# Attention into a gated MLP on one core: a new opening for the first head pair, and other places for two weight conversions

## Chip, core and metric

The kernel runs on 1 core of one Trainium2 chip. The metric is the device time of one execution in microseconds (us); lower is better. Times of the kernel before: 728.61, 730.03 and 730.19 us, median 730.03.

## What is computed

Rotary attention for 4 batches of 8 heads, 576 positions and head size 64, then a gated MLP on the result, all in FP32:

```python
q_rot, k_rot = (rotate(q), rotate(k))
scores = scale * np.matmul(q_rot, k_rot.transpose(0, 1, 3, 2))
scores = scores - np.max(scores, axis=-1, keepdims=True)
attn = np.exp(scores)
attn = attn / (np.sum(attn, axis=-1, keepdims=True) + 1e-09)
attn_out = np.matmul(attn, v)
...
x = np.ascontiguousarray(attn_out.transpose(0, 2, 1, 3)).reshape(B * S, H * D)
g = x @ w_gate
out = (g * (1.0 / (1.0 + np.exp(-g))) * (x @ w_val)) @ w_out
```

w_gate and w_val are 512 by 1536 float64 arrays, w_out 1536 by 512; the kernel reads their 64-bit words and converts them on the chip.

## The kernel before

The 32 heads are taken as 16 pairs. A pair's scores make 9 blocks of 128 queries by 576 keys: blocks 0 to 7 are four row groups i times the two heads h, block 8 holds the last 64 queries of both heads. Over all pairs the blocks are numbered n = 0 to 143, so n = 9 begins the second pair; here pairs are counted from 0.

**Per pair.** SP loads X (q and k, line 169) and VR (v, line 180). POOL turns q and k into rot (`turn`, lines 202 to 204). PE transposes rot (lines 281 and 285), ACT casts it to the high part of N (line 300), DVE subtracts to get the low part (line 304). FP32 products are made of three terms of high and low parts. SP then copies N into stacked tiles QK, QZ and BD (`qk_stack`, lines 311 to 318), which put a high and a low part in one contraction of 128 rows.

**Per block.** PE makes the scores (line 341): a block listed in `PLAN["direct"]` reads N alone, with 64 rows, three terms and six matmuls; any other of blocks 0 to 7 reads QK and QZ, with four. DVE takes the row maximum (`peak`, line 356), ACT the exponential (line 374), PE transposes E (line 417), ACT and DVE split it (lines 418 and 419), PE multiplies with the split v in VS (line 457), ACT evacuates (line 462) and SP stores Y (lines 476 to 482). The score tile sc has two buffers, so the scores of block n+2 wait for the exponential of block n. POOL makes VS from VR (`vsplit`, lines 270 and 271); VR has one buffer.

**The first weight block.** While attention runs, `wfirst(0, i)` loads a [128, 1024] piece of w_gate (i = 0) or w_val (i = 1) into a tile R (line 745) and `bits10` converts it in nine steps: ACT takes the absolute value (line 727), DVE makes four passes (lines 728 to 731), ACT casts the high part (line 703), DVE makes a fifth pass (line 732), POOL subtracts and adds (lines 705 and 706). R has one buffer; attention's row sums, too, are read back into R (line 611, from block 42 on).

**What sets the order.** `start` is written out by hand. Warming products (line 225, identity times identity into an unused tile) stand between its PE instructions, their counts in PLAN["warm"]. After it a loop over n calls one step function after another in PLAN["order"]; PLAN["cv"] holds, for each weight half, the n of the load and then of its nine steps. PE keeps program order while n < 9, SP while n < 27, POOL always; elsewhere a scheduler places the instructions. Each engine, and SP's queue of DMA starts, works strictly in the order shown.

After attention come the MLP's products: a plain part, a part with seven products in place of eight, and the down projection.

Of the kernel before, what the change touches and what calls it, by code (L numbers as in the profile page):

```python
# [24 lines left out]
NFF = DFF // 128  # L25
QH = 1216
PLAN = dict(
    direct=[0, 1, 2, 3, 4, 5, 9, 10],
    trb=3,
    warm=[10, 2, 2, 3, 2, 3],  # L30
    order=["qk", "scores", "trans", "pv", "exp", "evac", "rstore", "rope", "tails", "conv", "x", "conv1", "vsplit"],
    qk=[[3, 4, 6], [1, 2, 3], [0, 0, 1]],
    qkw=[[0, 2, 1], [2, 0, 1], [2, 0, 1]],
# [5 lines left out]
    rope=1,  # L39
    vsplit=8,  # L40
    rstore=0,
    cv=[[13, 16, 17, 21, 22, 23, 25, 25, 26, 26], [27, 29, 30, 30, 31, 32, 34, 34, 35, 35]],
    xs=[[4, 6], [5, 5], [6, 5], [7, 5], [8, 7], [9, 5], [10, 5], [11, 5], [12, 7], [13, 7], [14, 1], [14, 2],
        [14, 8], [15, 0], [15, 2], [15, 4]],
    xe=[[5, 3], [6, 3], [7, 3], [8, 3], [9, 3], [10, 3], [11, 3], [12, 3], [13, 5], [14, 1], [14, 3], [14, 5],
# [50 lines left out]
def r32(ap):  # L96
    return ap.bitcast(FP32)
# [10 lines left out]
class Attn:  # L108
# [103 lines left out]
    def start(self):  # L212
        nc = self.nc
        ve, po = nc.vector, nc.gpsimd
        rot = self.rot[0] = self.rot_p.tile([128, NSLOT, D], FP32, name="rot")
        rf = rot.rearrange("p s d -> p (s d)")
        T = nc.tensor.transpose
        tr = lambda: self.tr_p.tile([128, 512], FP32, name="tr")
        hi = lambda *x: self.qk_hi(0, *x)
        lo = lambda *x: self.qk_lo(0, *x)  # L220
        pw = self.pv_p.tile([128, 512], FP32, name="pv")

        def warm(n):
            for _ in range(n):
                nc.tensor.matmul(pw[:, 0:128], self.ident, self.ident, start=True, stop=True)  # L225
        w = PLAN["warm"]
        nc.scalar.copy(self.et_p.tile([128, 640], FP32, name="Et")[:, 0:1], r32(self.BD[0])[:, 0, 0:1])
        warm(w[0])
        self.turn(po, 0, 2)
        self.turn(ve, 0, 1, 0, 4, False)  # L230
        nc.scalar.mul(self.tab[0], self.tab[1], float(D ** -0.5))
        self.turn(ve, 0, 0, 0, 1)
        self.turn(po, 0, 0, 1, 4)
        pk, pt, pq = tr(), tr(), tr()
        kt = lambda i: T(pk[:, i * 128:(i + 1) * 128], rf[:, 512 + i * 128:640 + i * 128], self.ident)
        for o in (64, 0):
            T(pt[:, o:o + 128], rf[:, 1024:1152], self.ident)
        warm(w[1])
        for i in range(4):
            kt(i)  # L240
        warm(w[2])
        T(pq[:, 0:128], rf[:, 0:128], self.ident)
        for x in ((pt, None, 192), (pk, 640, 512), (pq, 64, 128)):
            hi(*x)
        for x in ((pt, None, 192), (pk, 640, 512), (pq, 64, 128)):
            lo(*x)
        nc.scalar.copy(self.VS[0][:, :, 0:64], self.VR)
        warm(w[3])
        self.scores(0, False, lambda x: warm(w[4]) if x == 0 else None)
        self.peak(0)  # L250
        self.scores(1, False)
        self.peak(1)
        self.exp(0)
        ps = tr()
        for i in range(1, 4):
            T(ps[:, i * 128:(i + 1) * 128], rf[:, i * 128:(i + 1) * 128], self.ident)
        warm(w[5])
        hi(ps[:, 128:512], 192, 384)
        lo(ps[:, 128:512], 192, 384)
        self.exp(1)  # L260
        del self.rot[0], self.X[0]
        self.load_qk(2)
        self.qk_stack(0)
# [56 lines left out]
    def scores(self, n, peak=True, then=None):  # L320
        nc = self.nc
        p, blk = divmod(n, 9)
        QK, BD, N = (t[p % 2] for t in (self.QK, self.BD, self.N))
        ps = self.sc_p.tile([128, 1024], FP32, name="sc").rearrange("p (a b) -> p a b", a=2)
        self.sc[n] = ps
        if n in PLAN["direct"]:
            i, h = divmod(blk, 2)
            sl = slice(64 + i * 128, 192 + i * 128)
            hs, ko = slice(64 * h, 64 * h + 64), (640, 576)[h]
            terms = [(N[hs, x, sl], N[hs, y], ko) for x, y in ((1, 1), (0, 1), (1, 0))]  # L330
        elif blk < 8:
            i, h = divmod(blk, 2)
            sl = slice(64 + i * 128, 192 + i * 128)
            ko = (640, 576)[h]
            QZ = self.QZ[p % 2]
            terms = [(QK[:, h, 0, sl], QK[:, h, 1], 0), (QZ[:, h, i * 128:(i + 1) * 128], N[:, 0], ko)]
        else:
            terms = [(BD[:, 1], N[:, 1], 640), (BD[:, 0], N[:, 1], 640), (BD[:, 1], N[:, 0], 640)]
        for x, (l, rr, o) in enumerate(terms):
            for g in range(2):  # L340
                nc.tensor.matmul(ps[:, g, 0:288], l, rr[:, o + g * 288:o + (g + 1) * 288],  # L341
                                 start=(x == 0), stop=(x == len(terms) - 1))
            if then:
                then(x)
        if peak:
            self.peak(n)
# [619 lines left out]
def attn_swiglu(ctx: ExitStack, tc: tile.TileContext, qk, vr, wg, wv, wo, main, tail, out):  # L966
# [6 lines left out]
    NB = NP * 9  # L973
# [4 lines left out]
    at = Attn(tc, actx, early, scx, qk, vr, (main, tail), yd, rd)  # L978
    ve, po = nc.vector, nc.gpsimd
# [17 lines left out]

    @step
    def scores(n, p, b):
        if 1 < n + 1 < NB:  # L1000
            at.scores(n + 1)

    @step
# [3 lines left out]

    @step
    def exp(n, p, b):
        if 1 < n + 1 < NB:  # L1010
            at.exp(n + 1)

    @step
# [66 lines left out]
    for n in range(NB):  # L1080
        p, b = divmod(n, 9)
        if n == 9:
            ctl1.__exit__(None, None, None)
        if (p, b) == (NP - 1, 0):
            assert not cvq
            early.close()
            moe.open_early(mctx)
        if n == 27:
            ctl0.__exit__(None, None, None)
        if b == P["lqk"] and 0 < p < NP - 3:  # L1090
            at.load_qk(p + 3)
        if b == P["lv"] and 0 < p < NP - 1:
            at.load_v(p + 1)
        for name in P["order"]:
            steps[name](n, p, b)
            if name == "qk" and n == P["qk"][0][2]:
                at.load_v(1)
                at.load_qk(3)
    assert not pend and not xq
    ctl2 = tc.manual_schedule(engines={getattr(mybir.EngineType, e) for e in ("PE", "Activation", "DVE", "SP")})  # L1100
# [4 lines left out]
    ps = [moe.mm(0, 0, 0, 0)]  # L1105
# [9 lines left out]
    ps = [moe.mm(0, 0, 1, 0)]  # L1115
# [258 lines left out]
```

## Time and profile before

| | |
|---|---|
| median of 3 runs | 730.03 us |
| profiled execution, its own time | 730.19 us |
| its span (first to last instruction) | 728.4 us |
| PE (TensorE) busy | 702.2 us, 96% |
| DVE (VectorE), POOL (GpSimd), ACT (ScalarE) busy | 542.7, 468.1, 408.7 us |
| DMA | 143.86 MB, mean 198 GB/s |

The profile is of one execution. All positions are us from the span's start, and lie 1.79 us short of that execution's own time. PE's ends are modelled, and its 128-column FP32 products show as two records each.

### The profile page before, as it was taken

To read this page: it belongs to the slowest core of one execution; us is meant where nothing else is said; L and a number is where in the kernel's file an instruction comes from. 1 tells how busy PE (TensorE), PEld (TensorE's weight loads), DVE (VectorE), ACT (ScalarE), POOL (GpSimd) and SP (SyncE) were. 2 spreads that over 40 slices of the span, in tenths; PEclk is the share of its full clock that TensorE was granted. 3 is DMA by queue.
4 is the path that set the end of the run, shared out by engine and by line. 5 is a ranking of instruction groups with operands and counts; after the bars stand their busy time and mean duration, and the time that the engine had idled before them with its cause. 6 is when DMAs were issued, how large, how long until landed. Compare 5 with 4: busy or idle time off the path is not lost.

```text
span 728.4 us, 12775 instructions
## 1 busy us (share of the span) xinstructions
PE 702.2 (96%) x4360; PEld 659.8 (91%) x4360; DVE 542.7 (75%) x888; ACT 408.7 (56%) x889; POOL 468.1 (64%) x469
## 2 busy tenths in 40 slices
PE   7979999999999999998999999999999999999997
PEld 7878889999999999997989999999999977888887
DVE  5878888898888889657988878777766894456451
ACT  4778788888888888446553434424334342343331
POOL 7885679999999966585976765556764857200000
PEclk9999999999999999999999999999999999999999
DMA  5787877879888878783346564755547974687661
GB/s 169 189 224 188 229 181 197 224 211 238 214 210 209 217 195 243 181 254 137 106 142 194 169 189 135 202 164 174 160 140 216 312 267 161 275 266 269 204 216 30
DMA packets 111329, 143.86 MB, mean 198 GB/s; under 512 B 17808, under 2 KB 86048, under 8 KB 111264
## 3 DMA queue, kind: packets, MB, share of 16 engines
q1 hardware_dynamic: 106576, 137.64, 65.8%
q10 hardware_dynamic: 4688, 5.39, 2.3%
q8 instruction: 35, 0.57, 0.3%
q14 instruction: 30, 0.25, 0.1%
HBM read 76.35 MB, written 42.54 MB: 163 GB/s over the span
## 4 chain that ended last, share of the span: by engine, by line
PE 67%; DMA 11%; DVE 7%; ACT 6%; POOL 3%; issue 3%; SPq 2%; ACTq 0%; POOLq 0%; DVEq 0%
PE ch L816 28%; PE ch L933 13%; PE pv L457 8%; PE sc L341 7%; PE tr L417 6%; PE ch L884 3%; DMA HF<-hf 2%; DMA QK<-N 2%; ACT E L374 2%; DMA raw<-in_moe_w_gate_dram 2%; DMA raw<-in_moe_w_val_dram 1%; DMA ht<-sv 1%; PE tr L281 1%; ACT N L300 1%; PE pv L225 1%
## 5 line engine op out<-in xcount | busy, mean ns | idle before, releaser
L356 DVE TENSOR_REDUCE nmt<-sc 128x1 f32<-128x576 f32 x144 | 108.0, 751 | 23.8 <-PE sc L341 22.7
L374 ACT ACTIVATE E<-sc,nmt 128x576 f32<-128x576 f32 x128 | 97.2, 759 | 4.2 <-DVE nmt L356 3.2
L417 PE MATMUL tr<-ident,E 128*128 128x128 f32 x512 | 77.6, 275 | 1.0 <-DVE ET1l L419 0.7
L800 POOL TENSOR_TENSOR u<-u,z 128x384 f32<-128x384 f32 x30 | 30.5, 1017 | 72.9 <-DVE sg L800 72.9
L417 PEld LDWEIGHTS tr<-ident,E 128*128 128x128 f32 x512 | 61.5, 141 | 4.1 <-PE tr L281 1.6
L341 PE MATMUL sc<-QK 128*128 128x288 f32 x240 | 59.1, 327 | 3.2 <-ACT E L374 1.9
L819 ACT COPY c<-ch 128x384 f32<-128x384 f32 x30 | 14.4, 480 | 84.7 <-PE ch L816 46.1
L202 POOL TENSOR_TENSOR t<-X,tab 128x256 f32<-128x256 f32 (+2 forms) x94 | 53.7, 593 | 5.9 <-DVE rot L204 3.4
L418 ACT CAST ET2h<-tr 128x512 fp32r<-128x512 f32 x80 | 47.0, 588 | 16.4 <-PE tr L417 16.0
L676 DVE TENSOR_TENSOR hl<-hg,hh 128x384 fp32r<-128x384 f32 x44 | 26.2, 595 | 38.9 <-ACT hh L676 38.9
L419 DVE TENSOR_TENSOR ET2l<-tr,ET2h 128x512 fp32r<-128x512 f32 x80 | 53.1, 681 | 2.1 <-ACT ET2h L418 2.0
L933 PE MATMUL ch<-Oh,hh 128*128 128x512 f32 (+1 forms) x144 | 54.0, 375 | 0.0
L933 PE MATMUL ch<-Oh,hl 128*128 128x512 f32 (+1 forms) x144 | 53.9, 374 | 0.0
L933 PE MATMUL ch<-Ol,hh 128*128 128x512 f32 (+1 forms) x144 | 53.8, 374 | 0.0
L341 PE MATMUL sc<-N,QZ 128*128 128x288 f32 x240 | 51.6, 297 | 0.0
L419 DVE TENSOR_TENSOR ET1l<-tr,ET1h 128x512 fp32r<-128x512 f32 x64 | 42.9, 685 | 9.3 <-ACT ET1h L418 9.0
L204 POOL TENSOR_TENSOR rot<-rot,t 128x512 f32<-128x512 f32 (+2 forms) x47 | 47.0, 999 | 3.7
L203 POOL TENSOR_TENSOR rot<-X,tab 128x512 f32<-128x512 f32 (+2 forms) x47 | 47.0, 1001 | 0.0
L676 ACT CAST hh<-hg 128x384 fp32r<-128x384 f32 x44 | 22.6, 513 | 41.4 <-DVE hg L920 41.4
L800 DVE TENSOR_TENSOR sg<-ch,u 128x384 f32<-128x384 f32 x60 | 33.4, 557 | 16.3 <-PE ch L816 13.3
L418 ACT CAST ET1h<-tr 128x512 fp32r<-128x512 f32 x64 | 36.6, 596 | 14.7 <-PE tr L417 14.5
L457 PE MATMUL pv<-ET2h,VS 128*128 128x320 f32 x128 | 41.1, 331 | 3.9 <-ACT ET2h L418 3.7
(414 smaller groups left out, 2415.9 us busy)
## 6 DMA issues: line engine op xcount, KB each, us to landing
QK<-N SPq DMA_DIRECT2D x64, 288.0 KB, 4.8
hg<-ht SPq DMA_DIRECT2D x22, 768.0 KB, 6.7
HF<-hf SPq DMA_DIRECT2D x12, 896.0 KB, 5.3
X<-in_qk_dram SPq DMA_DIRECT2D x15, 576.0 KB, 5.4
yd<-Y SPq DMA_DIRECT2D x31, 256.0 KB, 3.3
ht<-sg SPq DMA_DIRECT2D x20, 384.0 KB, 3.8
hf<-sg SPq DMA_DIRECT2D x20, 384.0 KB, 3.4
ht<-sg SPq DMA_DIRECT2D x20, 320.0 KB, 3.0
```

The costliest lines, as they stand in the source:

```text
L202: e.tensor_tensor(out=sel(t2, u), in0=sel(x, w), in1=tb(Sn, u), op=ALU.mult)
L341: nc.tensor.matmul(ps[:, g, 0:288], l, rr[:, o + g * 288:o + (g + 1) * 288], start=(x == 0), stop=(x == len(terms) - 1))
L356: nc.vector.tensor_reduce(out=nmcol, in_=ps[:, :, 0:288], axis=AX.XY, op=ALU.max, negate=True)
L374: nc.scalar.activation(out=E.rearrange("p (a b) -> p a b", a=2), in_=ps[:, :, 0:288], func=ACTF.Exp, bias=nmcol, scale=1.0, accum_out=self ...
L417: nc.tensor.transpose(ps[:, c], E[:, o + c * 128:o + (c + 1) * 128], self.ident)
L418: nc.scalar.copy(dst[0], src)
L419: nc.vector.tensor_tensor(out=dst[1], in0=src, in1=r32(dst[0]), op=ALU.subtract)
L457: nc.tensor.matmul(st["ps"][:, 0:w], VS[:, sl, :], t, start=(x == 0), stop=(x == last))
L676: return [lambda: self.nc.scalar.copy(h, f), lambda: le.tensor_tensor(out=l, in0=f, in1=r32(h), op=ALU.subtract)]
L800: add = lambda e, out, in0, in1: e.tensor_tensor(out=out, in0=in0, in1=in1, op=ALU.add)
L816: nc.tensor.matmul(acc, l[:, w, c * 128:(c + 1) * 128], r, start=(n == 0), stop=(n == 5))
L933: self.nc.tensor.matmul(ps, l[:, f], r[:, z], start=(n == 0), stop=(n == 3 * NFF - 1))
```

## The change

- The start's second row group of q gets its own turn on POOL (slots 1 to 2, then 2 to 4), its own transpose, cast and low part; row groups 2 and 3 follow after the scores of block 2, which move, with their exponential, from the loop into `start`.
- The warming counts go from 10, 2, 2, 3, 2, 3 (22 products) to 9, 0, 1, 2, 0, 1 (13).
- In directly read blocks the term (q high, k low) comes before (q low, k high).
- Block 11 is read directly from N. It is the one new entry of that table.
- The load of pair 1's v comes ahead of that pair's stacking copies on SP (n = 5), no longer behind them.
- The w_gate piece is loaded at n = 9 in place of 13, and its steps stand at n = 14 to 27 (before 16 to 26). The w_val piece is loaded at n = 29 (before 27), its steps at 33 to 41 (before 29 to 35).

```diff
--- before.py
+++ after.py
@@ -25,9 +25,9 @@
 NFF = DFF // 128
 QH = 1216
 PLAN = dict(
-    direct=[0, 1, 2, 3, 4, 5, 9, 10],
+    direct=[0, 1, 2, 3, 4, 5, 9, 10, 11],
     trb=3,
-    warm=[10, 2, 2, 3, 2, 3],
+    warm=[9, 0, 1, 2, 0, 1],
     order=["qk", "scores", "trans", "pv", "exp", "evac", "rstore", "rope", "tails", "conv", "x", "conv1", "vsplit"],
     qk=[[3, 4, 6], [1, 2, 3], [0, 0, 1]],
     qkw=[[0, 2, 1], [2, 0, 1], [2, 0, 1]],
@@ -39,7 +39,7 @@
     rope=1,
     vsplit=8,
     rstore=0,
-    cv=[[13, 16, 17, 21, 22, 23, 25, 25, 26, 26], [27, 29, 30, 30, 31, 32, 34, 34, 35, 35]],
+    cv=[[9, 14, 16, 17, 21, 22, 22, 25, 27, 27], [29, 33, 34, 35, 39, 39, 40, 40, 41, 41]],
     xs=[[4, 6], [5, 5], [6, 5], [7, 5], [8, 7], [9, 5], [10, 5], [11, 5], [12, 7], [13, 7], [14, 1], [14, 2],
         [14, 8], [15, 0], [15, 2], [15, 4]],
     xe=[[5, 3], [6, 3], [7, 3], [8, 3], [9, 3], [10, 3], [11, 3], [12, 3], [13, 5], [14, 1], [14, 3], [14, 5],
@@ -230,7 +230,8 @@
         self.turn(ve, 0, 1, 0, 4, False)
         nc.scalar.mul(self.tab[0], self.tab[1], float(D ** -0.5))
         self.turn(ve, 0, 0, 0, 1)
-        self.turn(po, 0, 0, 1, 4)
+        self.turn(po, 0, 0, 1, 2)
+        self.turn(po, 0, 0, 2, 4)
         pk, pt, pq = tr(), tr(), tr()
         kt = lambda i: T(pk[:, i * 128:(i + 1) * 128], rf[:, 512 + i * 128:640 + i * 128], self.ident)
         for o in (64, 0):
@@ -248,16 +249,21 @@
         warm(w[3])
         self.scores(0, False, lambda x: warm(w[4]) if x == 0 else None)
         self.peak(0)
+        T(pq[:, 128:256], rf[:, 128:256], self.ident)
         self.scores(1, False)
         self.peak(1)
+        hi(pq[:, 128:256], 192, 128)
         self.exp(0)
+        lo(pq[:, 128:256], 192, 128)
+        self.exp(1)
+        warm(w[5])
+        self.scores(2)
         ps = tr()
-        for i in range(1, 4):
+        for i in range(2, 4):
             T(ps[:, i * 128:(i + 1) * 128], rf[:, i * 128:(i + 1) * 128], self.ident)
-        warm(w[5])
-        hi(ps[:, 128:512], 192, 384)
-        lo(ps[:, 128:512], 192, 384)
-        self.exp(1)
+        hi(ps[:, 256:512], 320, 256)
+        lo(ps[:, 256:512], 320, 256)
+        self.exp(2)
         del self.rot[0], self.X[0]
         self.load_qk(2)
         self.qk_stack(0)
@@ -327,7 +333,7 @@
             i, h = divmod(blk, 2)
             sl = slice(64 + i * 128, 192 + i * 128)
             hs, ko = slice(64 * h, 64 * h + 64), (640, 576)[h]
-            terms = [(N[hs, x, sl], N[hs, y], ko) for x, y in ((1, 1), (0, 1), (1, 0))]
+            terms = [(N[hs, x, sl], N[hs, y], ko) for x, y in ((1, 1), (1, 0), (0, 1))]
         elif blk < 8:
             i, h = divmod(blk, 2)
             sl = slice(64 + i * 128, 192 + i * 128)
@@ -997,7 +1003,7 @@
 
     @step
     def scores(n, p, b):
-        if 1 < n + 1 < NB:
+        if 2 < n + 1 < NB:
             at.scores(n + 1)
 
     @step
@@ -1007,7 +1013,7 @@
 
     @step
     def exp(n, p, b):
-        if 1 < n + 1 < NB:
+        if 2 < n + 1 < NB:
             at.exp(n + 1)
 
     @step
@@ -1087,6 +1093,8 @@
             moe.open_early(mctx)
         if n == 27:
             ctl0.__exit__(None, None, None)
+        if n == 5:
+            at.load_v(1)
         if b == P["lqk"] and 0 < p < NP - 3:
             at.load_qk(p + 3)
         if b == P["lv"] and 0 < p < NP - 1:
@@ -1094,7 +1102,6 @@
         for name in P["order"]:
             steps[name](n, p, b)
             if name == "qk" and n == P["qk"][0][2]:
-                at.load_v(1)
                 at.load_qk(3)
     assert not pend and not xq
     ctl2 = tc.manual_schedule(engines={getattr(mybir.EngineType, e) for e in ("PE", "Activation", "DVE", "SP")})
```

**PE, first instructions of the program.** pv<-ident are the warming products, tr<-ident,rot transposes of q and k, sc<-N the directly read scores (six to a block), tr<-ident,E those of block 0. Before:

```order
L225 MATMUL pv<-ident 128x128 x10
L237 MATMUL tr<-ident,rot 128x128 x2
L225 MATMUL pv<-ident 128x128 x2
L235 MATMUL tr<-ident,rot 128x128 x4
L225 MATMUL pv<-ident 128x128 x2
L242 MATMUL tr<-ident,rot 128x128
L225 MATMUL pv<-ident 128x128 x3
L341 MATMUL sc<-N_93 128x288 x2
L225 MATMUL pv<-ident 128x128 x2
L341 MATMUL sc<-N_93 128x288 x10
L256 MATMUL tr<-ident,rot 128x128 x3
L225 MATMUL pv<-ident 128x128 x3
L341 MATMUL sc<-N_93 128x288 x6
L417 MATMUL tr<-ident,E 128x128 x4
```

Now:

```order
L225 MATMUL pv<-ident 128x128 x9
L238 MATMUL tr<-ident,rot 128x128 x2
L236 MATMUL tr<-ident,rot 128x128 x4
L225 MATMUL pv<-ident 128x128
L243 MATMUL tr<-ident,rot 128x128
L225 MATMUL pv<-ident 128x128 x2
L347 MATMUL sc<-N_93 128x288 x6
L252 MATMUL tr<-ident,rot 128x128
L347 MATMUL sc<-N_93 128x288 x6
L225 MATMUL pv<-ident 128x128
L347 MATMUL sc<-N_93 128x288 x6
L263 MATMUL tr<-ident,rot 128x128 x2
L423 MATMUL tr<-ident,E 128x128 x4
```

The scores of block 0 have two warming products just ahead of them and none inside; the last two transposes of q stand behind the scores of block 2 instead of ahead of them.

**SP, around the load of w_gate.** The names with 93 to 96 belong to even pairs, those with 113 to 116 to odd ones. Before, behind the stacking copies of pair 2:

```order
L318 DMA BD_95<-N_93 64x2x64
L180 DMA VR<-in_vr_dram 128x640
L481 DMA yd_57<-Y_538 128x2x256
L482 DMA yd_57<-Y_538 128x2x64
L745 DMA R<-in_moe_w_gate_dram 128x1024
L618 DMA Xab<-yd_57 64x2x384
L476 DMA yd_57<-Y_672 128x2x256
```

Now, behind those of pair 1:

```order
L324 DMA BD_115<-N_113 64x2x64
L169 DMA X<-in_qk_dram 128x1152
L482 DMA yd_57<-Y_401 128x2x256
L169 DMA X<-in_qk_dram 128x1152
L751 DMA R<-in_moe_w_gate_dram 128x1024
L317 DMA QK_94<-N_93 64x2x576
L318 DMA QK_94<-N_93 64x2x576
```

The load stands ahead of pair 2's eight stacking copies and of pair 3's load of v.

**SP, around the load of w_val and the stacking copies of pair 4.** Before:

```order
L618 DMA Xab<-yd_57 64x2x384 x2
L476 DMA yd_57<-Y_923 128x2x256
L313 DMA QZ_96<-N_93 64x512
L316 DMA QZ_96<-N_93 64x512
L317 DMA BD_95<-N_93 64x2x64
L745 DMA R<-in_moe_w_val_dram 128x1024
L318 DMA BD_95<-N_93 64x2x64
L180 DMA VR<-in_vr_dram 128x640
L311 DMA QK_94<-N_93 64x2x576
L312 DMA QK_94<-N_93 64x2x576
```

Now:

```order
L624 DMA Xab<-yd_57 64x2x384 x2
L180 DMA VR<-in_vr_dram 128x640
L482 DMA yd_57<-Y_924 128x2x256
L751 DMA R<-in_moe_w_val_dram 128x1024
L319 DMA QZ_96<-N_93 64x512
L322 DMA QZ_96<-N_93 64x512
L323 DMA BD_95<-N_93 64x2x64
L324 DMA BD_95<-N_93 64x2x64
L317 DMA QK_94<-N_93 64x2x576
L318 DMA QK_94<-N_93 64x2x576
```

The loads of VR and of w_val now stand ahead of all eight copies.

## Rows read from the trace of the kernel before

**Rows 1.** The page's busy table: each engine's busy time, share of the span and instructions.

```profile
PE 702.2 (96%) x4360; PEld 659.8 (91%) x4360; DVE 542.7 (75%) x888; ACT 408.7 (56%) x889; POOL 468.1 (64%) x469
```

**Rows 2.** Stretch table of three pairs: length; busy us (instructions) by engine; clock; DMA; GB/s.

```profile
49.60:73.40 23.80, 18.22 (x133) 17.27 (x131) 17.24 (x30) 17.26 (x42) 15.03 (x17) 0.93 0.74 201
73.40:94.40 21.00, 18.97 (x137) 16.82 (x135) 18.02 (x32) 16.12 (x40) 13.52 (x15) 1.00 0.73 199
110.70:127.20 16.50, 16.38 (x132) 15.97 (x130) 14.44 (x24) 14.61 (x38) 15.78 (x19) 1.00 0.75 187
```

**Rows 3.** Timeline of PE, 50 to 89 us: start, length, what [idle before <-releaser].

```profile
54.24 0.46 PE L457 MATMUL pv<-ET2h,VS 128*128 128x320 f32 x1 [3.69 <-ACT ET2h L418]
...
72.15 0.63 PE L417 MATMUL tr<-ident,Et 128*128 128x128 f32 x4 [1.54 <-DVE ET2l L419]
...
88.39 0.42 PE L341 MATMUL sc<-QK 128*128 128x288 f32 x2
```

**Rows 4.** Timeline of ACT, 52 to 81 us.

```profile
53.05 0.66 ACT L727 ACTIVATE R<-R 128x512 f32<-128x512 f32 x1 [4.10 <-DMA R<-in_moe_w_gate_dram]
...
69.19 0.68 ACT L703 CAST w0h<-R 128x512 fp32r<-128x512 f32 x1
...
80.20 0.67 ACT L727 ACTIVATE R<-R 128x512 f32<-128x512 f32 x1 [1.65 <-DMA R<-in_moe_w_val_dram]
```

**Rows 5.** Stretch table around PE's longest stop and at the start.

```profile
54.20:57.70 3.50, 3.19 (x12) 2.89 (x13) 2.92 (x5) 2.82 (x8) 3.42 (x4) 0.54 0.78 236
3.00:6.75 3.75, 3.70 (x17) 3.70 (x18) 1.43 (x4) 0.78 (x2) 1.88 (x5) 1.00 1.00 352
6.75:8.75 2.00, 2.00 (x20) 2.00 (x19) 1.65 (x6) 0.67 (x2) 0.35 (x1) 1.00 0.31 127
```

**Rows 6.** Timeline of SP's queue, 30 to 82 us.

```profile
33.01 0.41 SPq L169 DMA_DIRECT2D X<-in_qk_dram  x1
38.01 0.60 SPq L311 DMA_DIRECT2D QK<-N  x1
...
47.52 0.52 SPq L745 DMA_DIRECT2D R<-in_moe_w_gate_dram  x1
...
75.00 1.53 SPq L745 DMA_DIRECT2D R<-in_moe_w_val_dram  x1
...
80.56 1.47 SPq L315 DMA_DIRECT2D QK<-N  x1
```

**Rows 7.** Stretch table of DVE's instructions on tile R alone.

```profile
49.60:73.40 23.80, 3.05 (x5) 0.93 0.74 201
73.40:94.40 21.00, 3.32 (x5) 1.00 0.73 199
```

**Rows 8.** Chain of waits, 0 to 45 us: start, length, what.

```profile
8.92 0.67 PE pv L225 x6
...
10.05 0.64 PE pv L225 x4
...
12.23 0.83 ACT E L374 x2
13.07 0.37 ACT N L300
...
17.41 5.63 DMA QK<-N
...
23.18 0.77 PE sc L341 x4
...
27.99 0.99 PE sc L341 x6
...
34.37 0.53 PE sc L341 x4
```

**Rows 9.** Timeline of POOL, 8 to 72 us.

```profile
8.40 1.14 POOL L202 TENSOR_TENSOR t<-X,tab 128x192 f32<-128x192 f32 x2 [3.44 <-DVE rot L204]
...
71.33 1.30 POOL L706 TENSOR_TENSOR w0l<-R 128x512 fp32r<-128x512 f32 x1
```

## Prediction

> **What bounds the kernel now.** The page's busy table comes first: PE is busy for 702.2 us of the span, 96%, no other engine above 75% [rows 1]. So nearly every microsecond in which PE stops is a microsecond of the total, and work put on another engine costs nothing until PE waits for it. The next view is the stretch table, cut where pairs end. An undisturbed pair takes 16.5 us for 132 PE instructions, 0.125 us each; DVE is busy for 14.44 us of it [rows 2]. Two early stretches stand out: 23.8 us for 133 instructions, where 16.6 would do, and 21.0 us for 137, where 17.1 would do [rows 2]. They lost 7.2 and 3.9 us. These are the pairs in which w_gate and w_val are converted.
>
> The timelines say how. PE stood still for 3.69 us up to 54.24, released by ACT [rows 3]; ACT had itself stood for 4.10 us in front of the absolute value of w_gate, whose data had not landed [rows 4]. SP had only started that load at 47.52, 5.5 us before it was used [rows 6]. PE then ran at a mean granted clock of 0.54 from 54.2 to 57.7 [rows 5], which costs 3.5 x (1 - 0.54) = 1.6 us more: of its two levels it was mostly at 1.2 GHz in place of 2.4, after that stop. The second stop is 1.54 us before 72.15, behind DVE's low part [rows 3]; the cast of w_gate, 0.68 us, had just been put in front of the casts of that chain on ACT [rows 4]. Together 3.69 + 1.6 + 1.54 = 6.8 of the 7.2 us. In the next stretch ACT stood again, 1.65 us, for w_val, started at 75.00 [rows 4, 6], while DVE had 3.32 us of passes over R to do [rows 7] and was busy for 18.02 of 21.0 us [rows 2].
>
> **The change, step by step.** The sum is made against the profiled execution's 730.19 us, 0.16 above the median of 730.03.
>
> *The load of w_gate.* It now stands on SP right behind the load of X that started at 33.01 and took 0.41 [rows 6], so it starts near 33.5 and, with the same 5.5 us, lands near 39; two X loads ahead of it may make that 41. Its first step stands eleven ACT instructions earlier than before. It was reached at 53.05 - 4.10 = 48.95 [rows 4]; eleven instructions of some 0.55 us put it near 43. The wait is gone and with it the fall of the clock: -3.69 - 1.6 = -5.3. The cast stands a few blocks earlier, and the casts of the 72.15 chain keep the order of an undisturbed pair: -1.5.
>
> *The load of w_val and its steps.* The load keeps about its place in time, but its first step is four blocks later, n = 33 in place of 29; a block is 16.5 / 9 = 1.8 us, so the wait of 1.65 goes. All nine steps leave the 21.0 us stretch but the first three: -3.9 for that stretch, what comes back being the next item.
>
> *The DVE passes, now spread.* Ten passes of 3.05 + 3.32 = 6.4 us [rows 7] lie over four pairs, 1.6 each, where an undisturbed pair leaves 16.5 - 14.44 = 2.06 [rows 2]. The lower bound is 0. The upper is the 21.0 us stretch without its 1.65: 2.25 lost for 3.32 of passes, 0.68 per us, 4.3 in all. I take 2.0, under the middle, since each pair stays within its room: +2.0.
>
> *Block 11 read directly.* Six matmuls take 0.99, the four stacked ones 0.53 [rows 8]: +0.46. What it covers: the load of v ahead of pair 1's copies makes SP wait for POOL's `vsplit` and puts those copies back, by 0.7 at most as I estimate. Block 11 no longer needs them, and block 12 comes a block, 1.8 us, later. I cost the moved load at 0; without block 11's change it would cost up to 0.7.
>
> *The start.* One product less ahead of block 0's scores (0.67 for three [rows 8]), two less ahead of k's transposes, two less inside the scores (0.64 [rows 8]): block 0's exponential, at 12.23, comes about 1.2 earlier, at 11.0, and, being 0.83 long, ends near 11.85 [rows 8]. The scores of block 2 need its buffer and take 0.99, to 12.85. Only then come the transposes of q's last two row groups and their cast, some 0.8 together, to 13.65. Before, the one cast of all three groups ended at 13.07 + 0.37 = 13.44 [rows 8]. The stacking copies wait for exactly that cast; their chain ends with a copy started at 17.41 that took 5.63 us, and PE took up the scores of block 7 at 23.18, on its landing [rows 8]. So what PE gains at the start it loses in front of blocks 6 and 7, and the copies start 0.2 later: +0.2. Bounds: -0.7 if the cast comes 0.5 earlier and the 0.2 is saved as well, +1.5 if block 0 gains nothing, or the clock stays low there (below). POOL's split turn is four more instructions, where the two of rows 9 took 1.14: some 0.8 us, covered by its idle time (15.03 busy of 23.8 [rows 2]); uncovered it would be 0.8. The changed order of the two terms is worth at most tenths there, and stands in these bounds.
>
> Sum: -5.3 - 1.5 - 3.9 + 2.0 + 0.46 + 0.2 = -8.0, so 730.19 - 8.0 = **722.1 us**. Everything behind the sixth pair keeps its order and moves up whole.
>
> **The clock at the start.** From 3.0 to 6.75 PE got through 17 product records in 3.70 us, from 6.75 on through 20 in 2.0 [rows 5], so it begins at half speed even though the clock column reads 1.00 there. Nine of the 22 products that kept PE busy are gone, and between 7 and 9 us transposes and pauses replace most of them. By the rows the clock is lost after a stop of 3.69 us, not after one of 1.54 [rows 3, 5], and the new pauses are about 1 us: I let it stay at 2.4 GHz. The Trainium skill, page "TensorE: Matmul & The Clock Gate", part 4 on PE-mode transpose, says that transposes do not count as PE being busy in the way products do. By that rule the start would run at 1.2 GHz for longer, the second rival below; no row of this trace separates the two, since products stood between all transposes.
>
> **Rivals.**
> 1. *DVE gives back all of it.* For: DVE lost PE time in the 21.0 us stretch. Against: it then had all five passes of a half in one pair. 722.1 + 2.3 = 724.4 us.
> 2. *The clock stays low at the start.* Six us at half speed cost 3; half is hidden ahead of blocks 6 and 7, the rest makes the cast late: 722.1 + 1.5 = 723.6 us.
> 3. *The first load still lands late*, so that the change doesn't do what it is arranged for: SP may stand at the X load ahead of it, which waits for POOL. Against: a margin of 2 to 4 us. With the whole stop left, 722.1 + 5.3 = 727.4 us.
> 4. *SP stands at the w_val load, and the kernel is slower.* That load needs R, which POOL frees with its last step on w_gate; that ended at 72.63 before [rows 9] and, PE being 6.8 us earlier and a `vsplit` now ahead of it, should end near 67. Behind the load stand all eight copies of pair 4. From the load to the last copy read by block 37 took 5.56 us [rows 6]; with the rest of the issue and 5.63 to land that is 80. Pair 4's scores began at 88.39 [rows 3] and now come near 79.5, block 37 near 81: just in time. Every us by which POOL is later than 67 stops PE for about as long, and a long stop costs the 1.6 of clock too. From 73.5 on the whole gain is gone; at 75 it is 722.1 + 8 + 1.6 = 731.7 us. Against: POOL waited before for ACT's cast, which now comes five blocks ahead of POOL's step.
>
> The words of the change speak of three more unstacked blocks; the table gains one, block 11, and I priced one. Two more would be 0.9 us.
>
> **How the numbers follow.** Forecast 0.66, rivals 0.12, 0.10, 0.06 and 0.06. The range goes from 718.8 (nothing given back, 2.0; the start's lower bound, 0.9 below my value; the last 0.4 of the 7.2) to 727.0 (give-back and start both at their upper bounds make 725.7; short of rival 3 in full). A measurement of this kernel tells 0.2%, 1.5 us, from no change. Faster by more: 0.66 + 0.12 + 0.10 and most of rival 3, 0.92. Within: 0.04, the ends of rivals 3 and 4. Slower: 0.04, the rest of rival 4.
>
> **What would show it.** Right: no ACT wait on either weight load; the pair that took 23.8 us near 17; the clock column at 1.00 all through 40 to 70; block 7 beginning within 0.5 us of 23.2 behind a wait for QK of 1 to 2 us; DVE above 90% busy in four pairs with PE stops under 1 us; the last pairs and the MLP 8 us earlier and otherwise alike. Wrong: a PE stop over 3 us left anywhere before 110, block 7 much earlier than 23 us, or pairs 1 to 4 each losing over 1 us to DVE.

## Result and the profile after

The changed kernel takes 722.17 us (median of 4 runs, 720.41 to 724.69) against 730.11 us (4 runs, 728.61 to 733.0): a ratio of 0.9889, with a 95% interval from 0.9842 to 0.9936, so 1.1% faster. Run again it gave 723.00 us (6 runs) against 730.28 us (11 runs), ratio 0.9898 [0.9864, 0.9931]. The forecast was 722.1. The sum came out; not all of its terms did, and this section shows which.

The profiled execution took 723.66 us, its span 721.8, 6.6 less than before's 728.4. The line of the busy table that answers to [rows 1]:

```profile
PE 698.6 (97%) x4344; PEld 656.6 (91%) x4344; DVE 540.0 (75%) x889; ACT 410.0 (57%) x890; POOL 470.5 (65%) x473
```

PE still bounds the kernel. To see where the time went, both traces are cut at the same piece of work: the start of each pair's block 8, the only one read from the tile BD. Four pairs of before, from pair 1's block 8 to pair 5's (stretch table, columns as in [rows 2]):

```profile
43.36:65.88 22.52, 18.43 (x131) 17.27 (x130) 15.98 (x27) 15.40 (x38) 15.55 (x18) 0.92 0.84 212
65.88:85.87 19.99, 17.06 (x131) 15.95 (x130) 15.88 (x27) 16.16 (x40) 14.28 (x16) 1.00 0.78 216
85.87:104.00 18.13, 17.49 (x131) 16.14 (x131) 17.15 (x31) 15.86 (x41) 11.73 (x15) 1.00 0.62 158
104.00:121.42 17.42, 16.82 (x132) 16.03 (x131) 14.36 (x24) 14.69 (x38) 14.39 (x17) 1.00 0.90 227
```

The same four of the changed kernel:

```profile
43.84:60.98 17.14, 16.68 (x131) 15.90 (x130) 15.52 (x26) 15.64 (x39) 13.21 (x16) 1.00 0.82 202
60.98:78.59 17.61, 16.87 (x131) 16.02 (x130) 16.38 (x28) 15.58 (x39) 12.86 (x16) 1.00 0.91 233
78.59:99.69 21.10, 18.38 (x133) 17.61 (x131) 16.31 (x28) 15.48 (x39) 15.93 (x18) 0.92 0.78 209
99.69:116.56 16.87, 16.55 (x131) 15.93 (x130) 15.51 (x27) 15.45 (x39) 15.73 (x19) 1.00 0.89 214
```

The first pair gives back 5.4 us and has its full clock; the second 2.4. The third is a surprise: 3.0 us longer than before, with the clock down. The whole span, with a second profile of each kernel (among the experiments below), in us:

| stretch | before | before, 2nd | after | after, 2nd |
|---|---|---|---|---|
| start to pair 0's block 8 | 25.41 | 25.96 | 25.67 | 25.69 |
| to pair 1's | 17.95 | 17.96 | 18.17 | 18.16 |
| to pair 2's | 22.52 | 22.66 | 17.14 | 17.14 |
| to pair 3's | 19.99 | 19.99 | 17.61 | 18.13 |
| to pair 4's | 18.13 | 18.14 | 21.10 | 19.12 |
| to pair 5's | 17.42 | 17.83 | 16.87 | 16.88 |
| to the MLP's first plain product | 167.39 | 168.23 | 167.59 | 166.60 |
| to the end | 439.59 | 439.43 | 437.65 | 437.78 |
| span | 728.4 | 730.2 | 721.8 | 719.5 |

The surprise stands in the timeline of PE of the changed kernel (source lines from L234 on are numbered one to eight higher than before: L341 is L347, L745 is L751):

```profile
65.45 0.50 PE L347 MATMUL sc<-QK 128*128 128x288 f32 x2 [0.67 <-ACT Et L383]
...
82.31 0.50 PE L347 MATMUL sc<-QK 128*128 128x288 f32 x2 [2.32 <-DMA QK<-N]
```

At 82.31 begins block 36, the first of pair 4, behind a stop of 2.32 us for its stacked copies. The stretch table around it:

```profile
80.00:82.00 2.00, 0.00 (x0) 0.00 (x0) 0.35 (x1) 1.33 (x4) 1.92 (x3) 1.00 1.02 226
82.00:84.00 2.00, 1.69 (x13) 1.72 (x14) 0.88 (x2) 0.45 (x1) 1.92 (x3) 0.94 0.91 202
84.00:86.00 2.00, 2.00 (x11) 2.00 (x10) 1.98 (x6) 1.44 (x6) 1.84 (x5) 0.50 1.01 332
86.00:88.00 2.00, 2.00 (x15) 1.98 (x14) 1.24 (x2) 0.69 (x3) 2.00 (x3) 0.71 0.67 237
```

PE did nothing from 80 to 82, and the granted clock read 0.50 from 84 to 86, the lower of its two levels, only some 2 us after PE had taken up work again: 2 x 0.50 + 2 x 0.29 + 2 x 0.06 = 1.7 us lost behind a stop of 2.32. The DMA share beside it is 1.02, so the 16 engines had no room left while the copies were under way. SP's queue shows what stood ahead of them:

```profile
69.24 0.35 SPq L180 DMA_DIRECT2D VR<-in_vr_dram  x1
69.68 0.38 SPq L482 DMA_DIRECT2D yd<-Y  x1
71.90 0.33 SPq L751 DMA_DIRECT2D R<-in_moe_w_val_dram  x1
72.28 0.82 SPq L319 DMA_DIRECT2D QZ<-N  x1
...
75.93 0.59 SPq L318 DMA_DIRECT2D QK<-N  x1
...
78.14 0.86 SPq L321 DMA_DIRECT2D QK<-N  x1
```

SP stands before the w_val load until 71.90, and all eight copies of pair 4 stand behind it. SP's own waits, and POOL's timeline, which says when R came free:

```profile
SPq L624 <- DMA yd<-Y: 3.0, 1, 3.0
SPq L751 <- POOL w0l L712: 1.8, 1, 1.8
```

```profile
66.82 0.72 POOL L276 TENSOR_SCALAR VS<-VR 128x640 fp32r<-128x640 f32 x1 [4.20 <-DMA VR<-in_vr_dram]
67.63 1.58 POOL L277 TENSOR_TENSOR VS<-VR,VS 128x640 fp32r<-128x640 f32 x1
69.16 1.32 POOL L711 TENSOR_TENSOR R<-R,w0h 128x512 f32<-128x512 f32 x1
70.56 1.31 POOL L712 TENSOR_TENSOR w0l<-R 128x512 fp32r<-128x512 f32 x1
```

POOL's last step on w_gate ends at 71.87, and SP goes on at 71.90. POOL was not waiting for ACT's cast any more, as it did in before's order; it stood 4.20 us at `vsplit`, for v, which is now ahead of those two steps. This is the chain of waits that the fourth rival of the prediction names. Whether it also sets the length of PE's stop is asked below.

At the start the changed kernel is where it was: block 7 begins at 23.20 (before 23.18 [rows 8]). PE, then ACT:

```profile
7.55 1.11 PE L236 MATMUL tr<-ident,rot 128*128 128x128 f32 x4
...
16.64 0.66 PE L287 MATMUL tr<-ident,rot 128*128 128x128 f32 x4 [0.60 <-POOL rot L204]
...
22.35 0.66 PE L287 MATMUL tr<-ident,rot 128*128 128x128 f32 x4 [0.51 <-POOL rot L204]
23.20 0.50 PE L347 MATMUL sc<-QK 128*128 128x288 f32 x2 [0.18 <-DMA QK<-N]
```

```profile
11.68 0.74 ACT L380 ACTIVATE E<-sc,nmt 128x576 f32<-128x576 f32 x1 [0.27 <-DVE nmt L362]
...
14.07 0.37 ACT L306 CAST N<-tr 128x256 fp32r<-128x256 f32 x1 [0.32 <-PE tr L263]
```

The four transposes of k take 1.11 us; between warming products, in the kernel before, they took 0.60. So PE is still at the lower level there, and exp(0) comes only 0.55 us earlier than the 12.23 of [rows 8]; the late cast ends at 14.44, a microsecond after before's 13.44.

### The profile page after: what moved, and what is told of

It reads as the page before. It is cut to its first block, busy times and chain, and to the rows that moved or that the text cites. A ratio compares the mean times of both kernels' runs of the same rounds, so it can differ in the third digit from the quotient of the medians.

```text
span 721.8 us, 12739 instructions
## 1 busy us (share of the span) xinstructions
PE 698.6 (97%) x4344; PEld 656.6 (91%) x4344; DVE 540.0 (75%) x889; ACT 410.0 (57%) x890; POOL 470.5 (65%) x473
## 4 chain that ended last, share of the span: by engine, by line
PE 71%; DMA 10%; DVE 8%; ACT 6%; issue 2%; SPq 2%; POOL 1%; ACTq 0%; DVEq 0%; POOLq 0%
PE ch L822 26%; PE ch L939 13%; PE pv L463 10%; PE sc L347 9%; PE tr L423 7%; DMA HF<-hf 3%; PE ch L774 2%; PE tr L287 2%; DMA raw<-in_moe_w_gate_dram 2%; DMA QK<-N 2%; ACT E L380 1%; DMA ht<-sv 1%; DVE HF L880 1%; POOL fl L682 1%; DVE nmt L362 1%
## 5 line engine op out<-in xcount | busy, mean ns | idle before, releaser
L347 PE MATMUL sc<-QK 128*128 128x288 f32 x238 | 58.5, 327 | 4.2 <-DMA QK<-N 2.5
L424 ACT CAST ET2h<-tr 128x512 fp32r<-128x512 f32 x80 | 47.1, 588 | 16.5 <-PE tr L423 16.2
L347 PE MATMUL sc<-N,QZ 128*128 128x288 f32 x238 | 51.4, 298 | 0.0
L347 PEld LDWEIGHTS sc<-QK 128*128 128x128 f32 x238 | 36.7, 191 | 7.1 <-ACT E L380 3.3
```

The source lines that it names most:

```text
L424: nc.scalar.copy(dst[0], src)
```

## Experiments

Runs of one kernel differ by several microseconds (28 of before's 29 runs on one chip lay between 723.8 and 733.5 us), so each verdict rests on the ratio of medians with its interval and, for the mechanism, on the stretch from one block 8 to the next, which repeats to 0.1 us wherever nothing stops.

**Which half of the conversion gives what.** The kernel before, with one new row of PLAN["cv"] or both; and the changed kernel with both old rows, so that only the start, block 11 and the load of v are new.

```diff
-cv=[[13, 16, 17, 21, 22, 23, 25, 25, 26, 26], [27, 29, 30, 30, 31, 32, 34, 34, 35, 35]],
+cv=[[9, 14, 16, 17, 21, 22, 22, 25, 27, 27], [29, 33, 34, 35, 39, 39, 40, 40, 41, 41]],
```

The first row alone in the kernel before:

> The kernel before with only w_gate's row of the table of conversions changed (load at block 9, steps at 14 to 27); the start, block 11 and w_val stay as before. Theory A (the early load of w_gate brings the gain): the wait of 4.1 us on ACT and the half-speed stretch after it are gone, and the time is 5 to 7 us below that of before, near 724. Theory B (the new start brings it): within 1.5 us of before. If the stacking copies of pair 4 come late whenever the pairs ahead are faster, a stop of about 2 us shows here too, ahead of block 36.

The second row alone in it:

> The kernel before with only w_val's row of the table changed (load at block 29, steps at 33 to 41). Theory A: the stop for w_gate ahead of 54 us stays (3.7 us and the half speed after it), the waits for w_val go; pairs 3 and 4 together lose about 2 us less than before: 727 to 729 against a median of 729.4. If w_val's place alone were the change's worth: 724 or less.

Both in it:

> The kernel before with both rows of the table of conversions changed and the start, block 11 and the early load of v left as before. Theory A (the conversions bring all, but only together: the first half alone ran into a wait of 6.3 us for w_val on ACT): within 2 us of the changed kernel, 721 to 724, no ACT wait over 1 us on either weight load. Theory B (the start brings a part): 725 or more.

Both old rows in the changed kernel:

> The changed kernel with both conversions put back to their old places; what is left is the start (row group turned apart, 13 warming products, block 2 in the start, the order of the two terms), block 11 read directly and the earlier load of v. Theory A: 0 to 1 us above before, 730 to 731, with block 7 beginning at 23.2 as before, and the wait for w_gate back at 4 us. Theory B: 4 us or more below before.

| kernel | median us | ratio [95%] | to pair 2's block 8 | to 3's | to 4's |
|---|---|---|---|---|---|
| first row only | 727.92 | 0.9973 [0.9943, 1.0002] | 18.10 | 25.64 | 17.64 |
| second row only | 726.29 | 0.9946 [0.9927, 0.9966] | 24.02 | 17.95 | 16.98 |
| both rows only | 724.35 | 0.9916 [0.9892, 0.9940] | 18.40 | 16.80 | 22.80 |
| all but the rows | 729.12 | 0.9978 [0.9949, 1.0008] | 23.01 | 18.59 | 18.11 |

With the first row alone a gain of 5 to 7 us had been expected; the median gains 1.5, and its interval takes in no change at all. The wait for w_gate shrinks to under 1 us, and the stretch to pair 2's block 8 is 4.4 us shorter than before's 22.52. But the next takes 25.64 us in place of 19.99: the work is ahead of its old time by then, the w_val load hardly (73.95 after 75.00), and ACT is at its first step 4 us sooner. ACT and PE of that kernel:

```profile
80.85 0.67 ACT L727 ACTIVATE R<-R 128x512 f32<-128x512 f32 x1 [6.32 <-DMA R<-in_moe_w_val_dram]
```

```profile
82.78 0.85 PE L341 MATMUL sc<-QK 128*128 128x288 f32 x2 [5.42 <-ACT E L374]
```

So the later first step of the second row is not worth only the 1.65 us that I read in the trace of before [rows 4]; it is also what keeps the first row's gain. With the second row alone the first wait is still there (PE stopped 4.01 us up to 54.60), its stretch is 1.5 us longer than before's, with a mean clock of 0.86 in place of 0.92, and the next two are 2.0 and 1.2 us shorter. With both, the stop for the stacked copies appears, 3.33 us on PE at 84.39, without any of the change's other parts: it belongs to the two rows. Both rows alone give 0.9916, which is not told apart from the changed kernel's 0.9889 and 0.9898; the other parts by themselves give 0.2%, which these runs cannot tell from nothing.

**Is the order on SP what stops block 36?** Three edits of the changed kernel, each meant to take that stop away. First, POOL frees R a block earlier, ahead of its `vsplit`:

```diff
-cv=[[9, 14, 16, 17, 21, 22, 22, 25, 27, 27],
+cv=[[9, 14, 16, 17, 21, 22, 22, 25, 26, 26],
```

> The changed kernel with the last two steps of w_gate (POOL) at block 26 in place of 27, so that POOL frees R before it waits for pair 3's v. Theory D (SP's load of w_val, and the eight copies of pair 4 behind it, start when POOL frees R): the load starts 2 to 4 us earlier than at 71.9, the stop of 2.3 us ahead of block 36 and the half speed after it shrink or go, 719 to 721. Theory C (the copies are late for another reason, such as their wait for N or for DMA): the stop stays above 1.5 us, 722.

Then blocks 36 and 37 don't read the stacked copies:

```diff
-direct=[0, 1, 2, 3, 4, 5, 9, 10, 11],
+direct=[0, 1, 2, 3, 4, 5, 9, 10, 11, 36, 37],
```

> The changed kernel with blocks 36 and 37 read directly from N too, so that pair 4's first two blocks need no stacking copy. Costs two times 0.46 us on PE. Theory A2 and C alike: the stop of 2.3 us ahead of block 36 and the half speed after it, some 4 us together, are gone, 719 to 720. If the stop is only moved to block 38, it is shorter than 1 us there.

And SP keeps program order up to block 32 in place of 27, which puts the w_val load behind the eight copies (and, as the trace shows, a load of X ahead of them):

```diff
-        if n == 27:
+        if n == 32:
             ctl0.__exit__(None, None, None)
```

> The changed kernel with SP held to program order up to block 32 in place of 27, which puts the load of w_val behind the eight stacking copies of pair 4 and these right behind the store ahead of them. Theory A2 (SP standing at w_val's load, which waits for POOL to free R, makes the copies late and PE stops for 2.3 us ahead of block 36, then runs at half speed): that stop is gone and the time is 3 to 4 us below the changed kernel, 718 to 719. Theory C (the copies are late because PE is early, wherever the load stands): no more than 1 us below it. ACT may wait up to 1 us for w_val, whose load now starts some 5 us later.

| kernel | median us | ratio [95%] | w_val load starts | longest QK wait | to pair 4's block 8 |
|---|---|---|---|---|---|
| changed | 722.17 | 0.9889 [0.9842, 0.9936] | 71.90 | 2.32 | 21.10 |
| changed, again (below) | 723.00 | 0.9898 [0.9864, 0.9931] | 72.54 | 1.04 | 19.12 |
| R a block earlier | 723.65 | 0.9913 [0.9881, 0.9945] | 69.69 | 0.9 | 19.27 |
| 36, 37 direct | 722.12 | 0.9890 [0.9849, 0.9931] | 72.45 | 1.28 | 18.52 |
| load behind the copies | 726.49 | 0.9962 [0.9936, 0.9987] | 83.51 | 1.69 | 25.65 |

With R a block earlier, POOL does its two steps ahead of `vsplit`:

```profile
62.37 1.31 POOL L711 TENSOR_TENSOR R<-R,w0h 128x512 f32<-128x512 f32 x1
65.13 1.29 POOL L712 TENSOR_TENSOR w0l<-R 128x512 fp32r<-128x512 f32 x1 [1.45 <-DVE R L738]
67.11 0.72 POOL L276 TENSOR_SCALAR VS<-VR 128x640 fp32r<-128x640 f32 x1 [0.69 <-DMA VR<-in_vr_dram]
```

R is free at 66.42, 5.45 us earlier, but the load starts only 2.2 us earlier, at 69.69: SP stands 3.0 us for yd ahead of it, as it did in the changed kernel. The stop shrinks to 0.9 us, the clock stays at 1.00, and the stretch to pair 4's block 8 gains 1.8 on the first profile of the changed kernel, but nothing on the second. Direct blocks end the wait ahead of block 36 (the 1.28 us is another, at 66.04). Neither moves the median beyond its interval, where 719 to 721 us had been expected.

Loading w_val behind the copies is a clear loss, where a gain of 3 to 4 us had been expected. The copies come late all the same (1.69 us). Line 318's, which block 36 waits for, starts 2.2 us sooner than in the changed kernel (73.72 against 75.93) and takes 11.0 us to land (SP's queue, and the landing of that copy):

```profile
73.01 0.62 SPq L317 DMA_DIRECT2D QK<-N  x1
73.72 0.61 SPq L318 DMA_DIRECT2D QK<-N  x1
...
83.51 0.35 SPq L751 DMA_DIRECT2D R<-in_moe_w_val_dram  x1
```

```profile
DMA to landing us min/median/max: 11.0/11.0/11.0
```

The edit had brought a load of X, 576 KB against the 512 KB of w_val, just ahead of them, at 72.50; in the changed kernel that load starts at 80.27, behind them. So this kernel is no clean test of the one load's place, but it refutes the theory that SP's stand at that load alone makes the copies late. ACT then waits for w_val, with all of PE behind it:

```profile
90.55 0.66 ACT L733 ACTIVATE R<-R 128x512 f32<-128x512 f32 x1 [7.93 <-DMA R<-in_moe_w_val_dram]
```

```profile
84.86 0.50 PE L347 MATMUL sc<-QK 128*128 128x288 f32 x2 [1.69 <-DMA QK<-N]
92.47 0.81 PE L347 MATMUL sc<-QK 128*128 128x288 f32 x2 [3.21 <-ACT Et L380]
```

**The start.** The changed kernel with the old counts of warming products:

```diff
-warm=[9, 0, 1, 2, 0, 1],
+warm=[10, 2, 2, 3, 2, 3],
```

> The changed kernel with the warming counts of before (22 products in place of 13). Theory E (the start's PE time is hidden ahead of blocks 6 and 7, and only the clock counts): PE reaches full speed by 7 us in place of 8.7, block 7 still begins within 0.5 us of 23.2, and the time stays within 1 us of the changed kernel, near 722. Rival (fewer products bring time): block 7 and the total 0.8 us or more later.

723.29 us, ratio 0.9901 [0.9877, 0.9925]: the same as the changed kernel's, as theory E has it. Its block 7 is not where the theory put it: the k transposes take 0.60 us again, but exp(0) comes at 12.43, the copies start at 15.50 (14.47 with the thinner set), block 7 begins at 25.05 in place of 23.20, and PE reaches pair 0's block 8 at 27.35, 1.7 us later in its one profile. That half fits the rival.

And the changed kernel without block 11 read directly:

```diff
-direct=[0, 1, 2, 3, 4, 5, 9, 10, 11],
+direct=[0, 1, 2, 3, 4, 5, 9, 10],
```

> The changed kernel with block 11 again read from the stacked copies. My sum had block 11's six products in place of four cost 0.46 us, and the copies of pair 1 put back by 0.7 at most. If that is right, pair 1's blocks wait 0 to 0.7 us for QK at block 11, and the start of pair 1's block 8 (43.84 in the first profile) moves by -0.5 to +0.3 us against the start of pair 0's: no difference that timing can tell, ratio to before within 0.003 of the changed kernel's. Rival: the load of v put ahead of the copies matters, and block 11 waits over 1 us for QK; then pair 1 is longer by 1 us or more.

723.19 us, ratio 0.9902 [0.9867, 0.9937]. From pair 0's block 8 to pair 1's it takes 17.95 us, the old figure; all eight profiles with block 11 direct show 18.16 to 18.17. So block 11 costs 0.2 us, and without it no block waits for the copies there. Its profile shows something else, at a place that the edit doesn't touch:

```profile
10.00:13.50 3.50, 3.45 (x19) 2.63 (x19) 1.75 (x4) 1.84 (x5) 3.27 (x6) 0.95 0.12 20
13.50:26.00 12.50, 12.50 (x50) 10.55 (x50) 6.95 (x11) 6.29 (x16) 11.95 (x18) 0.50 0.75 177
```

PE has work for all of 13.5 to 26 us and gets the lower clock. Since 3.05 it had stood still for 0.75 us at most. Pair 0's block 8 begins at 29.42 in place of 25.67, and this execution is the slowest of its six runs (726.62 us; the others 721.86 to 724.21). The kernel with the load behind the copies had it too, at 0.50 from 18 to 22 us, its block 8 at 27.43. The other six profiles with nine warming products less kept the clock, and so did all six with the old counts. The second rival is thus real, as a thing that happens in some executions. The four k transposes don't foretell it: they took 0.66 us in both of these, and 0.66 to 1.12 us in all eight profiles with the thinner set.

**Both remedies together, and each kernel once more.** R a block earlier and blocks 36, 37 direct, as in the two diffs above:

> Two steps put together that each shortened pair 3: w_gate's last two conversion steps one block earlier (R free sooner) and blocks 36 and 37 read without the stacked copies. If the stop ahead of block 36 is what pair 3 loses, pair 3 takes 17.5 to 18.5 us, no wait for QK over 1.3 us is left there and the clock stays at 1.00 from 75 to 95; over the changed kernel that is 2 to 3 us less before the MLP (pair 7 and on), ratio to before 0.984 to 0.990. Rival: pair 3's length is set by DVE, which has the passes over R, and by the two direct blocks' extra matmuls (0.46 each); then the pair stays at 19 us or more and the ratio at 0.988 to 0.992, no better than the changed kernel.

The changed kernel again:

> The changed kernel once more, for a closer interval and to see what of its profile repeats. My reading of the first profile: the stop of 2.32 us ahead of block 36 is built into the order on SP (the w_val load waits for POOL to free R, all eight copies stand behind it), so it shows again, between 1.0 and 3 us, with pair 3 at 19 to 21.5 us; the full granted clock through the plain part of the MLP (57.6 us there, where eight of the other nine profiles have the clock fall after the three short stops and take 58.9 to 61.2) was a matter of luck, so that stretch should now read 58.5 to 61. Rival: the plain part is shorter by the change itself, and reads 57.6 again. Ratio to before 0.987 to 0.993 by both.

The kernel before again:

> The kernel before, unchanged, profiled once more, to see which of its losses repeat. My reading: the losses in pairs 2 and 3 are built into its order, so pair 2 takes 22 to 24 us and pair 3 18 to 21.5, with a stop over 3 us behind the absolute value of w_gate; the MLP, which was 2 us longer in the first profile of before than in any of the others (439.6 us from its first plain product to the end, against 437.2 to 438.5), had a second fall of the clock between 360 and 380 that is chance, so that it now reads 437 to 438.5 and the clock there 1.00. Rival: the MLP of the kernel before is longer by itself, and reads 439 to 440 again, with the clock at 0.9 between 360 and 380; then some 2 us of the change's gain lie there and want a cause.

The combination takes 722.80 us, ratio 0.9900 [0.9867, 0.9933], beside 723.00 us, 0.9898 [0.9864, 0.9931], of the changed kernel in the same session. The stretch that took 21.10 us is down to 17.84, with the clock at 1.00 throughout, PE busy for all but 0.1 us and no wait for QK:

```profile
79.51:97.35 17.84, 17.75 (x136) 16.57 (x135) 16.05 (x29) 15.35 (x39) 12.09 (x15) 1.00 0.73 189
```

So the stop can be taken away, and the time doesn't show it: the changed kernel's second profile loses only 1.3 us more there, and that difference is gone again by the MLP (282.05 against 281.72). No version tried here beats the changed kernel by more than the runs can tell. In that second profile the stops ahead of pair 4 are shorter, though the load starts later (72.54), because the copy of line 317 landed in 3.7 us in place of 5.8:

```profile
81.56 0.50 PE L347 MATMUL sc<-QK 128*128 128x288 f32 x2 [1.04 <-DMA QK<-N]
84.46 0.50 PE L347 MATMUL sc<-QK 128*128 128x288 f32 x2 [0.30 <-DMA QK<-N]
```

The clock stayed at 1.00 behind these, and the stretch took 19.12 us. Line 317's copy started at 72.81 us with R a block earlier, at 75.24 in the changed kernel and at 76.36 in its second profile, and landed at 79.84, 81.02 and 80.10: its start moved by 3.6 us, its landing by 1.2, and not in step. So SP's stand at the w_val load is real, but no run shows that it sets the stop. The fastest landing, 3.7 us, went with the lowest DMA share from 76 to 81 us, 0.86 against 0.97 and 1.03; what decides the landing stays open. The Trainium skill, page "DMA: Bandwidth & Descriptors", section "Issuing engines are not separate DMA queues", says that transfers of all engines run on the same 16 DMA engines and interleave; the share of 0.91 to 1.02 from 80 to 86 us, while loads and copies were in flight together, agrees with it.

The plain part of the MLP took 61.2 us this time, in place of 57.6, so the full clock there in the first profile was luck; the MLP as a whole stayed within 0.2 us of the first.

The second profile of before refuted my reading of the MLP. I had put its 2 us there down to chance; they came again, 439.43 us after 439.59, and so did the fall of the clock (stretch table and PE of that profile):

```profile
360.00:380.00 20.00, 18.18 (x96) 17.86 (x96) 17.77 (x28) 11.00 (x15) 17.92 (x14) 0.91 0.45 133
```

```profile
368.93 0.46 PE L816 MATMUL ch<-T0l,W0h 128*128 128x384 f32 x1 [1.82 <-DVE T0l L676]
```

A stop of 1.8 us for DVE's low part of T0 stands there in both profiles of before, with the clock at 0.91 over the 20 us, (1 - 0.91) x 20 = 1.8 us. In the twelve other profiles the clock reads 1.00 there, also in the one with all but the rows, which has the same stop:

```profile
368.04 0.44 PE L822 MATMUL ch<-T0l,W0h 128*128 128x384 f32 x1 [1.81 <-DVE T0l L682]
```

From this product to the first of the down projection both profiles of before take 204.4 us, and that kernel and both profiles of the changed one 202.9: the fall itself costs 1.5 us.

## Why the prediction was right, and where it was not

*The load of w_gate, -5.3: right.* Its load starts at 33.70 (forecast near 33.5), ACT takes its first step at 43.22 (near 43) without a wait, and the clock is 1.00 from 43.84 to 78.59. The margin was thin: the load landed at 42.46, not at 39 to 41, 0.8 us ahead of its use and not 2 to 4, and four of the variants that load at block 9 waited 0.4 to 1.0 us there. The stretch that held the stop of 3.69 us is 5.4 us shorter in the first profiles, 5.5 in the second.

*The w_val half: the step of the sum that failed.* For the three stretches from pair 2's block 8 to pair 5's the sum had -1.5, -3.9 and +2.0, so -3.4. The first profiles show 0.0 (-2.4 + 3.0 - 0.6), the second -1.8. The stop of 1.54 us behind DVE's low part is gone; what failed is "-3.9 for that stretch", which took it that nothing would stand in the place of the steps moved away. Under it lies the estimate of the fourth rival that POOL "should end near 67": it ended at 71.87. I had moved POOL's steps up by PE's gain and had named the `vsplit` ahead of them, but priced it as work and not as a wait; it stood 4.20 us for v. The stop for the stacked copies comes with the two rows (both rows alone, 3.33 us) and goes when the first two blocks don't read the copies. That POOL's late release of R sets it, as the rival has it, is not shown: with R free 5.45 us earlier 0.9 us of the stop are left, beside 2.32 and 1.04 in the two profiles of the changed kernel, and with the load behind the copies 1.69. The rival's price was wrong too: R came 4.9 us later than 67, and PE stopped 2.32 and 1.04 us, not some 4.9. The 1.6 us of clock behind a long stop came as forecast, once in two profiles.

*DVE's passes, +2.0: right in size as far as it can be separated.* The three stretches without the long stop take 17.14, 17.61 and 16.87 us where 16.5 would do, 2.1 more in all. DVE is busy for 91 to 93% of them, and the longest PE stop in them is 0.67 us.

*Block 11, +0.46: it is +0.2*, by the eight profiles with and the kernel without. And the load of v ahead of the copies costs nothing that shows there.

*The start, +0.2: right by two errors.* Block 7 begins within 0.02 us of before and pair 0's block 8 0.3 us later or earlier. But the wait of 1 to 2 us for QK is not there (0.18): block 0's exponential came 0.55 us earlier and not 1.2, and PE waited twice for POOL's turn, 0.60 and 0.51, which I had taken as covered. "I let it stay at 2.4 GHz" was wrong for the first microseconds: PE reached that level later than before, and two executions of eight then lost it altogether, for 1.8 and 3.8 us. The rule of the Trainium skill on PE-mode transpose, which I weighed against it ("TensorE: Matmul & The Clock Gate", part 4), fits the 1.11 us of the k transposes better than my reading did. Whether transposes or simply fewer products made it so, no run here separates, nor why the same transposes took 0.66 us in the two executions that lost the level later.

*"Everything behind the sixth pair keeps its order and moves up whole": off by 1.7 to 1.9 us.* The MLP of the changed kernel is that much shorter, in both pairs of profiles, and 1.5 us of it are the fall of PE's clock behind the T0 stop, which it doesn't have. Why that fall shows in both profiles of the kernel before and in no variant, though one has the same stop, stays open.

So in the first profiles -8.0 was forecast and -6.6 measured, as -4.7 in attention and -1.9 in the MLP; in the second -10.7, as -9.0 and -1.7. The medians lie between, at -7.9 and -7.3. The forecast of the total is partly luck: the stretches behind pair 2 gave 1.6 to 3.4 us less than I said, and the MLP nearly 2 us that I hadn't seen.

## What to carry to other kernels

When a load is moved on an in-order queue, ask what frees its buffer, and then what stands ahead of *that* instruction on its own engine; here SP stood 1.8 us for a step of POOL, which had itself stood 4.2 us for a load, and eight copies stood behind. Then ask whether the transfers have room: with DMA shares of 0.86 to 1.03, a copy that started 3.6 us sooner landed only 0.3 us sooner. A wait that goes can come back one step on: moved alone, the first half's 4.4 us turned into a stop of 5.4 us for the other half's load. And a single profile is not a sum of steady terms: cut both traces at the same piece of work, take a second profile of each kernel, and only then say which differences repeat.

## What the runs showed of the hardware that I had not expected

The fall of the clock doesn't go by the length of one stop alone. It fell behind stops of 1.8 us (the MLP of before, twice) and 2.32 us; in another kernel it stayed behind the same 1.8 us stop, and in the changed kernel behind one of 2.04 us in the MLP, with the column at 1.00 over 340 to 360 us; and at the start it fell for 12 us in an execution whose PE had not stood still for more than 0.75 us. The line of that longer stop:

```profile
351.23 0.45 PE L822 MATMUL ch<-xa2h,W0h 128*128 128x384 f32 x1 [2.04 <-DVE u L806]
```

The prediction's rule of thumb, lost after 3.69 us and not after 1.54, was too simple. And a fall can show late: behind the 2.32 us stop the column read 0.94 in the first 2 us of work and 0.50 in the next 2.
